# Two thirds of a kernel's query and key transposes from TensorE to the DMA engines, a table built by a product, and wider weight rows

## The chip, the core and the metric

The kernel runs on one core of one Trainium2 chip. The time is the device time of a whole launch in microseconds (us). Some executions are over 1.5% slower than the fastest of the same kernel ("slow" runs, the others are "fast"). Every ratio compares "fast" runs with fast runs.

Engine names: PE is TensorE, PEld its weight load, DVE VectorE, ACT ScalarE, POOL GpSimd, SP (SyncE) the engine that issues most of the DMAs.

## The reference, cut to what matters

```python
# r, k, v: 4 x 8 heads x 768 steps x 48 channels, fp32;  w, u: 8 x 48
for t in range(S):
    cur = k_t (outer) v_t * u
    y[t] = r_t @ (state + cur)
    state = w * state + k_t (outer) v_t
x = y as (3072 tokens, 384)
h = x @ w_in                      # 384 -> 2048
g = maximum(0.01 * h, h)
out = g @ w_out                   # 2048 -> 384, fp32
```

## The kernel before

The recurrence is cut into 24 stages (4 batches of 6 chunks of 128 steps). A stage loads r, k and v (three loads of 192 KB in rows of 192 bytes), scales r and k by decay tables on DVE, transposes both on PE, evicts the transposes on ACT, takes the key-query product, masks it on DVE, multiplies by v and by the carried state, and transposes the result into `xT`. The feed-forward part works on `xT`: first products with w_in, leaky ReLU on ACT, second products with w_out. The first eight tiles have 128 tokens, one per stage; the last four have 512 tokens, so each needs four stages. A small list scheduler in the kernel sorts the operations of each engine by priority before the program is built. Every engine then runs its list strictly in order.

```python
def load(n):                       # three per stage, issued by SyncE; NRAW = 4 buffers
    op("SP", lambda ...: [SP.dma_start(raw[ri][:, :, :], src)], ..., w=[f"{nm}{ri}"])

def front(n):                      # stage n
    ... DVE: qh = r * qdec ;  kh = k * kdec ;  bonus with uw = w * u
    def tr():                      # 8 transposes of 128x128 on TensorE into p_t
        for x, t in ((0, qh), (1, kh)):
            for i in range(NP):
                last = PE.transpose(p_t[:, 512 * x + 128 * i: ... ], t[:, 2 * i:2 * i + 2, :], ident[:, :])
    op("PE", tr, ...)
    op("ACT", lambda: ACT.activation(T, p_t[:, :], AF.Copy), ...)     # eviction, 128x1024
    op("PE", at, ...)              # key-query product p_a <- T
    op("DVE", ...)                 # ATm_0, ATm_1 <- p_a * mask
    ... state update
# [...]
u_tab <- u copied to 128 partitions by one 192 KB load
w_in:  4 loads of fp32, 12 casts on ACT into w_in_sb[:, m, 512 * i: ...]
w_out: 8 casting loads issued by GpSimd, rows of 384 fp32, at WOUT_AT = [3, 3, 4, 4, 5, 5, 6, 6]
```

## Time and profile before

The kernel before takes 194.04 us (193.76 to 194.24, 4 runs). The next lines are from the profile page: PE's busy time with its share of the span of 191.5 us and its instructions, and then the busy tenths of three rows in 40 slices of the span (4.8 us each).

```profile
PE 170.2 (89%) x1768; PEld 113.7 (59%) x1768; DVE 109.3 (57%) x239; ACT 120.5 (63%) x212; POOL 28.8 (15%) x40
...
PE   0249778868899999999999999999999999999994
DVE  2578696977999999999998989910000000000000
DMA  4999999999998989999594010002200121011222
```

PE is full from about a third of the span on. DVE is full from there until two thirds, and the DMA engines are full from the start to slice 20. The stretches view gives the same as busy times in parts of the span; its columns are named in its first line.

```profile
core 0: us, PE busy (x) PEld busy (x) DVE busy (x) ACT busy (x) POOL busy (x), PEclk, DMA share, GB/s
0.00:52.00 52.00, 33.95 (x521) 29.48 (x521) 38.42 (x87) 36.41 (x64) 14.04 (x24) 0.97 1.00 208
...
64.00:92.00 28.00, 28.00 (x315) 18.59 (x313) 27.34 (x59) 15.18 (x28) 5.12 (x6) 1.00 0.98 211
92.00:128.00 36.00, 36.00 (x380) 21.77 (x380) 31.85 (x70) 31.13 (x55) 7.91 (x8) 1.00 0.26 57
```

In the first 52 us PE is busy 34 us, partly with slow instructions (a stage's eight transposes take 1.03 us at 6.9 us and 0.61 us at 53.5 us), while the DMA share is 1.00. (The share counts the time of the packets; they can overlap, so a share above 1 is possible, and it is no exact measure of a full engine.) From 64 to 92 us PE is busy all the time, DVE 27.3 of 28 us, and the DMA share is still 0.98. After 92 us the loads are done (share 0.26). The chain of waits (start, duration, what) agrees:

```profile
22.38 5.80 DMA gT<-in_moe_w_in_dram
28.20 1.68 ACT w_in_sb L484 x3
...
31.49 19.62 DMA raw_v<-in_v_dram x4
...
167.86 20.81 PE p_moe L541 x128
...
188.70 0.49 ACT o_sb L545
```

Early, the chain stands on the load of w_in and on 19.6 us of raw loads; late, it is TensorE alone.

The DMA queue lines of the page give packets, megabytes and the share of the engines' time; the second is GpSimd's queue, which carries w_out.

```profile
q1 hardware_dynamic: 80224, 22.42, 50.6%
q0 software_dynamic: 2176, 1.57, 5.8%
```

The share of w_out is 5.8% of 191.5 us, 11.1 us of all DMA engines.

### The profile page before, as it was taken

Reading aid. Unit: us, or ns where it says so; the run is one execution under the profiler, and the core shown is the slowest. Engines: PE = TensorE matmul, PEld = TensorE weight load, DVE = VectorE, ACT = ScalarE, POOL = GpSimd, SP = SyncE. Lnnn points to the kernel's source line nnn. Section 1 sums busy time; section 2 is a strip of 40 time slices with the busy share of each in tenths; the row PEclk is TensorE's granted clock in tenths of the full one; section 3 lists DMA queues with packets and bytes.
Section 4 is the critical chain, followed back from the end, with each engine's and each line's share of the span. In section 5 each row is a group of like instructions: output and inputs, shape, how many; then the busy total and the mean of one; then the engine's idle time right before and its main releaser. Section 6 shows DMA issues by size and latency. Waiting matters only on the chain.

```text
span 191.5 us, 4244 instructions
## 1 busy us (share of the span) xinstructions
PE 170.2 (89%) x1768; PEld 113.7 (59%) x1768; DVE 109.3 (57%) x239; ACT 120.5 (63%) x212; POOL 28.8 (15%) x40
## 2 busy tenths in 40 slices
PE   0249778868899999999999999999999999999994
PEld 0137667768899676666556656566544654456651
DVE  2578696977999999999998989910000000000000
ACT  3476996668798664554999879851497228922221
POOL 2011153423211111111122121300000000000000
PEclk9999996999999999999999999999999999999999
DMA  4999999999998989999594010002200121011222
GB/s 92 218 213 265 272 245 221 205 200 170 176 213 166 220 173 227 213 238 200 135 202 85 3 41 0 3 0 84 86 0 0 41 82 44 0 39 50 75 86 82
DMA packets 82835, 24.27 MB, mean 127 GB/s; under 512 B 75904, under 2 KB 81280, under 8 KB 82816
## 3 DMA queue, kind: packets, MB, share of 16 engines
q1 hardware_dynamic: 80224, 22.42, 50.6%
q0 software_dynamic: 2176, 1.57, 5.8%
q8 instruction: 14, 0.23, 0.5%
q10 hardware_dynamic: 416, 0.00, 0.1%
q14 instruction: 5, 0.04, 0.1%
HBM read 20.84 MB, written 4.72 MB: 133 GB/s over the span
## 4 chain that ended last, share of the span: by engine, by line
PE 69%; DMA 13%; SPq 11%; DVE 3%; ACT 2%; issue 1%
PE p_moe L541 33%; PE p_moe L521 25%; DMA raw_v<-in_v_dram 10%; SPq L374 8%; PE p_t L404 3%; DMA gT<-in_moe_w_in_dram 3%; PE p_a L415 3%; PE p_y L456 2%; PE p_y L450 2%; PE p_moe L466 1%; SPq L343 1%; SPq L480 1%; PE p_z L428 1%; ACT w_in_sb L484 1%; DVE y_sb L462 1%
## 5 line engine op out<-in xcount | busy, mean ns | idle before, releaser
L521 PE MATMUL p_moe<-xT,w_in_sb 128*128 128x128 bf16 (+1 forms) x576 | 75.4, 280 | 3.0 <-ACT gS L526 1.4
L521 PEld LDWEIGHTS p_moe<-xT,w_in_sb 128*128 128x128 bf16 x576 | 41.9, 102 | 22.5 <-ACT w_in_sb L484 1.9
L541 PE MATMUL p_moe<-w_out_sb,gT 128*128 128x384 bf16 x256 | 42.3, 326 | 0.0
L526 ACT ACTIVATE gT<-p_moe 128x512 bf16<-128x512 f32 x64 | 37.9, 599 | 4.2 <-PE p_moe L521 1.9
L545 ACT ACTIVATE o_sb<-p_moe 128x384 f32<-128x384 f32 x24 | 11.8, 491 | 36.9 <-PE p_moe L541 36.9
L541 PEld LDWEIGHTS p_moe<-w_out_sb,gT 128*128 128x128 bf16 x256 | 25.0, 98 | 16.7
L396 POOL TENSOR_TENSOR vs<-v_sb,s_b 128x384 f32<-128x384 bf16 x24 | 21.4, 893 | 86.2 <-DVE s_b L394 81.3
L409 ACT ACTIVATE qkT<-p_t 128x1024 bf16<-128x1024 bf16 x24 | 24.6, 1026 | 8.1 <-PE p_t L404 7.8
L541 PE MATMUL p_moe<-w_out_sb,gS 128*128 128x384 bf16 x128 | 24.6, 326 | 0.1
L388 ACT ACTIVATE v_sb<-raw_v 128x384 bf16<-128x384 f32 x24 | 12.5, 526 | 11.0 <-DMA raw_v<-in_v_dram 8.3
L526 ACT ACTIVATE gS<-p_moe 128x512 bf16<-128x512 f32 x32 | 18.0, 603 | 1.5 <-PE p_moe L521 1.2
L420 DVE TENSOR_TENSOR ATm_0<-p_a,mask_f 128x512 bf16<-128x512 f32 x24 | 16.4, 684 | 2.0 <-PE p_a L415 1.9
L384 DVE TENSOR_TENSOR q_h<-raw_r,qdec 128x384 bf16<-128x384 f32 x24 | 13.9, 580 | 5.6 <-ACT qdec L351 3.4
L420 DVE TENSOR_TENSOR ATm_1<-p_a,mask_f 128x512 bf16<-128x512 f32 x24 | 16.3, 681 | 0.0
L404 PE MATMUL p_t<-ident,q_h 128*128 128x128 bf16 x96 | 9.8, 227 | 7.3 <-DVE k_h L386 7.3
L386 DVE TENSOR_TENSOR k_h<-raw_k,kdec 128x384 bf16<-128x384 f32 x24 | 15.2, 632 | 0.3 <-DMA raw_k<-in_k_dram 0.3
L462 DVE TENSOR_TENSOR y_sb<-p_y,vs 128x384 bf16<-128x384 f32 x24 | 13.3, 555 | 3.5 <-PE p_y L456 3.3
L541 PEld LDWEIGHTS p_moe<-w_out_sb,gS 128*128 128x128 bf16 x128 | 11.3, 98 | 6.1 <-issue 0.2
L394 DVE TENSOR_REDUCE s_b<-qku 128x8 f32<-128x384 bf16 x24 | 13.1, 547 | 0.2
L470 ACT ACTIVATE xT<-p_moe 128x384 bf16<-128x384 bf16 x24 | 11.7, 489 | 1.6 <-PE p_moe L466 1.6
L404 PEld LDWEIGHTS p_t<-ident,q_h 128*128 128x128 bf16 x96 | 6.9, 102 | 9.2 <-DVE k_h L386 7.5
L415 PE MATMUL p_a<-qkT 64*128 64x128 bf16 x192 | 10.0, 226 | 2.3 <-ACT qkT L409 2.3
(42 smaller groups left out, 146.0 us busy)
## 6 DMA issues: line engine op xcount, KB each, us to landing
raw_r<-in_r_dram SPq DMA_DIRECT2D x24, 192.0 KB, 4.4
raw_k<-in_k_dram SPq DMA_DIRECT2D x24, 192.0 KB, 4.5
raw_v<-in_v_dram SPq DMA_DIRECT2D x24, 192.0 KB, 4.5
out_dram<-o_sb SPq DMA_DIRECT2D x24, 192.0 KB, 1.9
gT<-in_moe_w_in_dram SPq DMA_DIRECT2D x4, 768.0 KB, 5.8
w_out_sb<-in_moe_w_out_dram POOLq DMA_DIRECT2D x8, 192.0 KB, 4.9
w_tab<-in_w_dram SPq DMA_DIRECT2D x1, 192.0 KB, 3.6
u_tab<-in_u_dram SPq DMA_DIRECT2D x1, 192.0 KB, 5.8
```

What stands on the lines that cost most here:

```text
L374: op("SP", lambda src=src, raw=raw: [SP.dma_start(raw[ri][:, :, :], src)], 650, order[0], w=[f"{nm}{ri}"], dma=(f"{nm}{ri}", 16), svc=1000)
L384: op("DVE", lambda: V.tensor_tensor(qh[:, :, 0:D], rr[:, :, :], qdec[:, :, :], ALU.mult), 490, base + 2, w=[f"q{pi}"], r=[f"rr{ri}", "qdec ...
L386: op("DVE", lambda: V.tensor_tensor(kh[:, :, 0:D], rk_[:, :, :], kdec[:, :, :], ALU.mult), 490, base + 3, w=[f"k{pi}"], r=[f"rk{ri}", "kde ...
L396: op("POOL", lambda: G.tensor_tensor(vs[di][:, :, :], vv[:, :, :], s_b[di][:, :].unsqueeze(2).to_broadcast([128, H, D]), ALU.mult), 790, b ...
L404: last = PE.transpose(p_t[:, 512 * x + 128 * i:512 * x + 128 * i + 128], t[:, 2 * i:2 * i + 2, :].rearrange("p h e -> p (h e)"), ident[:, :])
L409: op("ACT", lambda: ACT.activation(T[:, :, :, :].rearrange("p a i t -> p (a i t)"), p_t[:, :], AF.Copy), 910, base + 9, w=[f"T{di}"], r=[g ...
L415: last = PE.matmul(p_a[p][:, 128 * i:128 * i + 128], T[64 * p:64 * p + 64, 1, i, :], T[64 * p:64 * p + 64, 0, i, :], start=True, stop=True)
L420: op("DVE", lambda p=p: V.tensor_tensor(ATm[di][p][:, :, :], p_a[p][:, :].rearrange("p (i t) -> p i t", t=L), mask_f[:, :].unsqueeze(1).to ...
L462: op("DVE", lambda: V.tensor_tensor(y_sb[di][:, :], p_y[:, 0:DM], vs[di][:, :, :].rearrange("p h d -> p (h d)"), ALU.add), 490, base + 15, ...
L521: op("PE", lambda m=m, fb=fb, gr=gr: PE.matmul(p_moe[gr.bank][:, nt * (fb % per):nt * (fb % per) + nt], w_in_sb[:, m, 128 * fb:128 * fb + ...
L526: op("ACT", lambda f0=f0, gr=gr: ACT.activation(gb[:, f0:f0 + per, :], p_moe[gr.bank][:, :].rearrange("p (f t) -> p f t", t=nt), AF.Lrelu) ...
L541: op("PE", lambda q=q, fb=fb, gr=gr: PE.matmul(p_moe[gr.bank][:, 0:DM], gb[:, fb, 128 * q:128 * q + 128], w_out_sb[:, fb, :], start=(fb == ...
```

## The change

It does four things:

1. From stage eight on (`NXQ = 8`), q and k are transposed by a DMA issued from SyncE instead of by PE. This saves the ACT eviction too. From the same stage on, a stage's loads wait until k of two stages earlier is done (`GATE = 2`).
2. u is loaded as one row and spread over the partitions by a one-row product on PE.
3. w_out is loaded in four DMAs whose rows hold four neighbouring rows (6144 bytes). This permutes the hidden channels, so w_in's columns are permuted in its casts.
4. There are four preparation buffers instead of three, three transpose buffers instead of two, and new ranks, priorities and DMA times for the scheduler. So every engine's order of work changes too. `FILL` and `NXY` are set so that they do nothing.

```diff
-WOUT_AT = [3, 3, 4, 4, 5, 5, 6, 6]
-NPREP = 3
+NXQ = 8 ; GATE = 2 ; NT = 3
+WOUT_AT = [3, 4, 5, 6]
+CAST = [20, 118, 160, 218]
+NPREP = 4
[...]
-    op("SP", lambda: [SP.dma_start(u_tab[:, :, :], dram_ap(u, 0, [[0, 128], [D, H], [1, D]]))], ...)
+    op("ACT", lambda: [ACT.dma_start(u_row[:, :], u.rearrange("h d -> (h d)").unsqueeze(0))], ...)
+    op("PE", lambda: PE.matmul(p_moe[gu.bank][:, 0:DM], ones_f[0:1, :], u_row[:, :], ...), ...)
[...]
             op("SP", lambda src=src, raw=raw: [SP.dma_start(raw[ri][:, :, :], src)], 650, order[0],
-               w=[f"{nm}{ri}"], dma=...)
+               w=[f"{nm}{ri}"], after=[f"k{(n - GATE) % NPREP}"] if n >= NXQ else [], dma=...)
[...]
+        if n < NXQ:
             op("PE", tr, ...) ; op("ACT", ... AF.Copy ...)        # as before
+        else:
+            op("SP", lambda: [SP.dma_start_transpose(T..., qk_h[pi]...)], 650, base + RANK["T"], ...)
[...]
-    wo_view = moe_w_out.rearrange("(s p) c -> p s c", p=128)
+    wo_view = moe_w_out.rearrange("(g p j) c -> p g j c", p=128, j=4)
[...]
-            op("ACT", ... w_in_sb[:, m, CH * i:CH * i + CH] <- w_st[i][:, m, :] ...)
+            op("ACT", ... w_in_sb[...].rearrange("p (j q) -> p j q", j=4)
+                       <- w_st[i][:, m, :].rearrange("p (q j) -> p j q", j=4) ...)
```

More of the change, by code (lines that the diff above doesn't have):

```diff
@@ L28 @@
 NRAW = 4
-WIN_AT = [0, 1, 2, 3]
-WOUT_AT = [3, 3, 4, 4, 5, 5, 6, 6]
-NPREP = 3
+FILL = (0.0, 0.0, 215.0)
+NT = 3
+GATE = 2
+NXQ = 8
+NXY = 24
+WIN_AT = [0, 1, 2, 3]
+WOUT_AT = [3, 4, 5, 6]
+CAST = [20, 118, 160, 218]
+RANK = {"q": 2, "k": 3, "v": 4, "bonus": 5, "vs": 7, "T": 8, "Tev": 9, "A": 10, "mask": 11, "kv": 10, "Z": 12, "S": 12,
+        "qs": 14, "av": 14, "y": 15, "xt": 16, "xev": 17}
+NPREP = 4
 NGT = 3
@@ L37 @@
 SLACK = 250
-DMA_LEAD = 1300
-DMA_TAIL = 700
+DMA_LEAD = 1800
+DMA_TAIL = 600
 class Op:
@@ L150, in schedule @@
             if not ready[e]:
+                if e == "PE" and FILL[0] <= free[e] and t < FILL[1] and t - free[e] > 2 * FILL[2]:
+                    o = self.filler(held, free[e])
+                    if o is not None:
+                        o.start, o.end = free[e], free[e] + o.dur
+                        free[e] += o.dur
+                        order[e].append(o)
+                        continue
                 free[e] = t
@@ L190, in schedule, with filler @@
         return order
+    def filler(self, held, t):
+        z = self.writer["zeros"]
+        if z.start is None or z.end > t:
+            return None
+        for b, g in enumerate(held["moe"]):
+            if g is None or (g.last.start is not None and g.last.end <= t):
+                gr = Group("moe")
+                gr.bank = b
+                o = self.op("PE", lambda: self.fill_fn(b), FILL[2], 0, w=[gr], r=["zeros"], grp=gr)
+                o.users = []
+                if g is not None:
+                    o.deps.add(g.last)
+                held["moe"][b] = gr
+                return o
+        return None
     def sync(self, nc, ctx):
@@ L284, in bass_rwkv5_eagle__then__act_leaky_relu_kernel @@
     kdec = SB("kdec", [128, H, D], FP32)
-    u_tab = SB("u_tab", [128, H, D], FP32)
+    u_row = SB("u_row", [1, DM], FP32)
     wt = SB("wt", [128, NP], FP32)
@@ L297, in bass_rwkv5_eagle__then__act_leaky_relu_kernel @@
     v_sb = [SB(f"v_sb{i}", [128, H, D]) for i in range(NPREP)]
-    q_h = [SB(f"q_h{i}", [128, H, E]) for i in range(NPREP)]
-    k_h = [SB(f"k_h{i}", [128, H, E]) for i in range(NPREP)]
+    qk_h = [SB(f"qk_h{i}", [128, 2, H, E]) for i in range(NPREP)]
+    q_h = [t[:, 0, :, :] for t in qk_h]
+    k_h = [t[:, 1, :, :] for t in qk_h]
     qk = [SB(f"qk{i}", [128, H, D]) for i in range(2)]
@@ L303, in bass_rwkv5_eagle__then__act_leaky_relu_kernel @@
     vs = [SB(f"vs{i}", [128, H, D], FP32) for i in range(2)]
-    qkT = [SB(f"qkT{i}", [128, 2, NP, L]) for i in range(2)]
+    qkT = [SB(f"qkT{i}", [128, 2, NP, L]) for i in range(NT)]
     ATm = [[SB(f"ATm{i}_{p}", [128, NP, L]) for p in range(2)] for i in range(2)]
@@ L321, in bass_rwkv5_eagle__then__act_leaky_relu_kernel @@
     p_z = PS("p_z")
+    zeros = SB("zeros", [128, 512])
     P = Prog({"moe": NMOE, "t": 1})
     op = P.op
+    P.fill_fn = lambda b: PE.matmul(p_moe[b][:, :], zeros[:, 0:128], zeros[:, :], start=True, stop=True)
+    op("DVE", lambda: V.memset(zeros[:, :], 0.0), 200, -101, w=["zeros"])
     op("ACT", lambda: ACT.preload_act_table_set("natural_log_exp_and_others"), 1300, -100, w=["acttab"])
@@ L333, in bass_rwkv5_eagle__then__act_leaky_relu_kernel @@
     op("SP", lambda: [SP.dma_start(w_tab[:, :, :], dram_ap(w, 0, [[0, 128], [D, H], [1, D]]))], 650, -100,
-       w=["w"], dma=("w", 16), svc=530)
+       w=["w"], dma=("w", 16), svc=900)
     op("DVE", lambda: V.memset(wt[:, :], 1.0), 70, -100, w=["wt"])
@@ L342, in bass_rwkv5_eagle__then__act_leaky_relu_kernel @@
     op("ACT", wt_dma, 1300, -99, w=["wt"], dma=("wt", 32), svc=300)
-    op("SP", lambda: [SP.dma_start(u_tab[:, :, :], dram_ap(u, 0, [[0, 128], [D, H], [1, D]]))], 650, 1.5,
-       w=["u"], dma=("u", 16), svc=530)
+    op("ACT", lambda: [ACT.dma_start(u_row[:, :], u.rearrange("h d -> (h d)").unsqueeze(0))], 650, -98.9,
+       w=["u"], dma=("u", 16), svc=100)
+    gu = Group("moe")
+    op("PE", lambda: PE.matmul(p_moe[gu.bank][:, 0:DM], ones_f[0:1, :], u_row[:, :], start=True, stop=True), 1300, -90,
+       w=[gu], r=["u", "ones"], grp=gu)
     op("DVE", lambda: V.tensor_reduce(trs[:, :], mask_f[:, :], AX.X, ALU.add), 220, -95, w=["trs"], r=["mask"])
@@ L360, in bass_rwkv5_eagle__then__act_leaky_relu_kernel @@
                                              AF.Exp, scale=float(L)), 250, -49, w=[f"wlm{p}"], r=["wt"])
-    op("DVE", lambda: V.tensor_tensor(uw[:, :, :], w_tab[:, :, :], u_tab[:, :, :], ALU.mult), 490, 3.5, w=["uw"],
-       r=["w", "u"])
+    op("DVE", lambda: V.tensor_tensor(uw[:, :, :], p_moe[gu.bank][:, 0:DM].rearrange("p (h d) -> p h d", d=D),
+                                      w_tab[:, :, :], ALU.mult), 490, -80, w=["uw"], r=["w", gu], grp=gu)
     for i in range(NPREP):
@@ L374, in load @@
             op("SP", lambda src=src, raw=raw: [SP.dma_start(raw[ri][:, :, :], src)], 650, order[0],
-               w=[f"{nm}{ri}"], dma=(f"{nm}{ri}", 16), svc=1000)
+               w=[f"{nm}{ri}"], after=[f"k{(n - GATE) % NPREP}"] if n >= NXQ else [], dma=(f"{nm}{ri}", 16), svc=1000)
             order[0] += 1
@@ L383, in front @@
         qh, kh = q_h[pi], k_h[pi]
-        op("DVE", lambda: V.tensor_tensor(qh[:, :, 0:D], rr[:, :, :], qdec[:, :, :], ALU.mult), 490, base + 2,
+        op("DVE", lambda: V.tensor_tensor(qh[:, :, 0:D], rr[:, :, :], qdec[:, :, :], ALU.mult), 490, base + RANK["q"],
            w=[f"q{pi}"], r=[f"rr{ri}", "qdec"], lock=True)
-        op("DVE", lambda: V.tensor_tensor(kh[:, :, 0:D], rk_[:, :, :], kdec[:, :, :], ALU.mult), 490, base + 3,
+        op("DVE", lambda: V.tensor_tensor(kh[:, :, 0:D], rk_[:, :, :], kdec[:, :, :], ALU.mult), 490, base + RANK["k"],
            w=[f"k{pi}"], r=[f"rk{ri}", "kdec"], lock=True)
-        op("ACT", lambda: ACT.activation(vv[:, :, :], rv[:, :, :], AF.Copy), 420, base + 4, w=[f"v{pi}"],
+        op("ACT", lambda: ACT.activation(vv[:, :, :], rv[:, :, :], AF.Copy), 420, base + RANK["v"], w=[f"v{pi}"],
            r=[f"rv{ri}", "acttab"])
-        op("DVE", lambda: V.tensor_tensor(qk[di][:, :, :], qh[:, :, 0:D], kh[:, :, 0:D], ALU.mult), 270, base + 5,
+        op("DVE", lambda: V.tensor_tensor(qk[di][:, :, :], qh[:, :, 0:D], kh[:, :, 0:D], ALU.mult), 270, base + RANK["bonus"],
            w=[f"qk{di}"], r=[f"q{pi}", f"k{pi}"], lock=True)
-        op("DVE", lambda: V.tensor_tensor(qku[di][:, :, :], qk[di][:, :, :], uw[:, :, :], ALU.mult), 270, base + 5,
+        op("DVE", lambda: V.tensor_tensor(qku[di][:, :, :], qk[di][:, :, :], uw[:, :, :], ALU.mult), 270, base + RANK["bonus"],
            w=[f"qku{di}"], r=[f"qk{di}", "uw"], lock=True)
-        op("DVE", lambda: V.tensor_reduce(s_b[di][:, :], qku[di][:, :, :], AX.X, ALU.add), 470, base + 6,
+        op("DVE", lambda: V.tensor_reduce(s_b[di][:, :], qku[di][:, :, :], AX.X, ALU.add), 470, base + RANK["bonus"],
            w=[f"s{di}"], r=[f"qku{di}"])
@@ L397, in front @@
                                           s_b[di][:, :].unsqueeze(2).to_broadcast([128, H, D]), ALU.mult), 790,
-           base + 7, w=[f"vs{di}"], r=[f"s{di}", f"v{pi}"], lock=True)
+           base + RANK["vs"], w=[f"vs{di}"], r=[f"s{di}", f"v{pi}"], lock=True)
+        T, ti = qkT[n % NT], n % NT
         gt = Group("t")
@@ L406, in tr @@
             return last
-        op("PE", tr, 450, base + 8, w=[gt], r=[f"q{pi}", f"k{pi}", f"qpad{pi}", f"kpad{pi}", "ident"], grp=gt)
-        T = qkT[di]
-        op("ACT", lambda: ACT.activation(T[:, :, :, :].rearrange("p a i t -> p (a i t)"), p_t[:, :], AF.Copy), 910,
-           base + 9, w=[f"T{di}"], r=[gt], grp=gt)
+        if n < NXQ:
+            op("PE", tr, 450, base + RANK["T"], w=[gt], r=[f"q{pi}", f"k{pi}", f"qpad{pi}", f"kpad{pi}", "ident"], grp=gt)
+            op("ACT", lambda: ACT.activation(T[:, :, :, :].rearrange("p a i t -> p (a i t)"), p_t[:, :], AF.Copy), 910,
+               base + RANK["Tev"], w=[f"T{ti}"], r=[gt], grp=gt)
+        else:
+            op("SP", lambda: [SP.dma_start_transpose(T[:, :, :, :].rearrange("p a i t -> p (a i) t"),
+                                                     qk_h[pi][:, :, :, :].rearrange("p a h e -> p (a h e)"))], 650,
+               base + RANK["T"], w=[f"T{ti}"], r=[f"q{pi}", f"k{pi}", f"qpad{pi}", f"kpad{pi}"], dma=(f"T{ti}", 16), svc=1500)
         def at():
@@ L417, in at @@
             return last
-        op("PE", at, 330, base + 10, w=["pa0", "pa1"], r=[f"T{di}"], banks=["a0", "a1"])
+        op("PE", at, 330, base + RANK["A"], w=["pa0", "pa1"], r=[f"T{ti}"], banks=["a0", "a1"])
         for p in range(2):
@@ L422, in front @@
                                                   mask_f[:, :].unsqueeze(1).to_broadcast([128, NP, L]), ALU.mult),
-               630, base + 11, w=[f"A{di}{p}"], r=[f"pa{p}", "mask"], banks=[f"a{p}"])
+               630, base + RANK["mask"], w=[f"A{di}{p}"], r=[f"pa{p}", "mask"], banks=[f"a{p}"])
         if c < NC - 1:
@@ L431, in kv @@
                 return last
-            op("PE", kv, 230, base + 10, w=["pz"], r=[f"k{pi}", f"kpad{pi}", f"v{pi}"], banks=["z"])
+            op("PE", kv, 230, base + RANK["kv"], w=["pz"], r=[f"k{pi}", f"kpad{pi}", f"v{pi}"], banks=["z"])
             pz = p_z[:, 0:DM].rearrange("p (i e) -> p i e", e=2 * D)
@@ L435, in front @@
             if c == 0:
-                op("DVE", lambda: V.tensor_tensor(s_bd[nxt][:, :, :], pz, wlm[:, :, :], ALU.mult), 490, base + 12,
+                op("DVE", lambda: V.tensor_tensor(s_bd[nxt][:, :, :], pz, wlm[:, :, :], ALU.mult), 490, base + RANK["Z"],
                    w=[f"sb{nxt}"], r=["pz", "wlm0", "wlm1"], banks=["z"])
@@ L439, in front @@
                 op("DVE", lambda: V.tensor_tensor(z_st[zi][:, :, :], pz, s_bd[cur][:, :, :], ALU.add), 490,
-                   base + 12, w=[f"z{zi}"], r=["pz", f"sb{cur}"], banks=["z"])
+                   base + RANK["Z"], w=[f"z{zi}"], r=["pz", f"sb{cur}"], banks=["z"])
                 op("DVE", lambda: V.tensor_tensor(s_bd[nxt][:, :, :], z_st[zi][:, :, :], wlm[:, :, :], ALU.mult),
-                   290, base + 12, w=[f"sb{nxt}"], r=[f"z{zi}", "wlm0", "wlm1"], lock=True)
+                   290, base + RANK["S"], w=[f"sb{nxt}"], r=[f"z{zi}", "wlm0", "wlm1"], lock=True)
     def back(n):
@@ L446, in back @@
         pi, di, sc, base = n % NPREP, n % 2, n % 3, n * 100
-        T, vv = qkT[di], v_sb[pi]
+        T, ti, vv = qkT[n % NT], n % NT, v_sb[pi]
         def qs():
@@ L459, in back @@
         if c > 0:
-            op("PE", qs, 200, base + 14, w=["py"], r=[f"T{di}", f"sb{sc}"], banks=["y"])
-        op("PE", av, 330, base + 14, w=["py"], r=[f"A{di}0", f"A{di}1", f"v{pi}"], banks=["y"])
+            op("PE", qs, 200, base + RANK["qs"], w=["py"], r=[f"T{ti}", f"sb{sc}"], banks=["y"])
+        op("PE", av, 330, base + RANK["av"], w=["py"], r=[f"A{di}0", f"A{di}1", f"v{pi}"], banks=["y"])
         op("DVE", lambda: V.tensor_tensor(y_sb[di][:, :], p_y[:, 0:DM], vs[di][:, :, :].rearrange("p h d -> p (h d)"),
-                                          ALU.add), 490, base + 15, w=[f"y{di}"], r=["py", f"vs{di}"], banks=["y"])
+                                          ALU.add), 490, base + RANK["y"], w=[f"y{di}"], r=["py", f"vs{di}"], banks=["y"])
         def xt():
@@ L468, in back @@
         gx = Group("moe")
-        op("PE", xt, 170, base + 16, w=[gx], r=[f"y{di}", "ident"], grp=gx)
-        op("ACT", lambda: ACT.activation(xT[:, :, L * n:L * n + L],
-                                         moe16(gx)[:, 0:DM].rearrange("p (m t) -> p m t", t=L), AF.Copy), 370,
-           base + 17, w=[f"x{n}"], r=[gx], grp=gx)
+        if n < NXY:
+            op("PE", xt, 170, base + RANK["xt"], w=[gx], r=[f"y{di}", "ident"], grp=gx)
+            op("ACT", lambda: ACT.activation(xT[:, :, L * n:L * n + L],
+                                             moe16(gx)[:, 0:DM].rearrange("p (m t) -> p m t", t=L), AF.Copy), 370,
+               base + RANK["xev"], w=[f"x{n}"], r=[gx], grp=gx)
+        else:
+            op("SP", lambda: [SP.dma_start_transpose(xT[:, :, L * n:L * n + L], y_sb[di][:, :])], 650, base + RANK["xt"],
+               w=[f"x{n}"], r=[f"y{di}"], dma=(f"x{di}", 16), svc=700)
     CH = DFF // 4
     wi_view = moe_w_in.rearrange("(m p) c -> p m c", p=128)
-    wo_view = moe_w_out.rearrange("(s p) c -> p s c", p=128)
+    wo_view = moe_w_out.rearrange("(g p j) c -> p g j c", p=128, j=4)
     def weights_in(i):
@@ L483, in weights_in @@
         for m in range(NSL):
-            op("ACT", lambda m=m: ACT.activation(w_in_sb[:, m, CH * i:CH * i + CH], w_st[i][:, m, :], AF.Copy), 520,
-               20 + i, w=[f"win{i}_{m}"], r=st + ["acttab"])
+            op("ACT", lambda m=m: ACT.activation(
+                w_in_sb[:, m, CH * i:CH * i + CH].rearrange("p (j q) -> p j q", j=4),
+                w_st[i][:, m, :].rearrange("p (q j) -> p j q", j=4), AF.Copy), 520,
+               CAST[i], w=[f"win{i}_{m}"], r=st + ["acttab"])
     def weights_out(i, after):
-        op("POOL", lambda: [G.dma_start(w_out_sb[:, 2 * i:2 * i + 2, :], wo_view[:, 2 * i:2 * i + 2, :])],
-           1000, 130 + 100 * i, w=[f"wout{i}"], after=after, dma=(f"wout{i}", 16), svc=1330)
+        op("POOL", lambda: [G.dma_start(w_out_sb[:, 4 * i:4 * i + 4, :], wo_view[:, i, :, :])],
+           1000, 130 + 100 * i, w=[f"wout{i}"], after=after, dma=(f"wout{i}", 16), svc=2100)
     def loads(n):
@@ L538, in g2 @@
             oi[0] += 1
-            ready = [f"{gk}_{fb}" for fb in range(NFB)] + [f"wout{j}" for j in range(8)]
+            ready = [f"{gk}_{fb}" for fb in range(NFB)] + [f"wout{j}" for j in range(4)]
             for fb in range(NFB):
```

## The prediction

> **What bounds it now.** The chain of waits has two parts. Until about 52 us it is input: SyncE issuing loads, a w_in load, and 19.6 us of raw loads ending at 51.1 us. From 63.4 to 188.7 us it is TensorE without a gap; the windows view shows PE busy 4.00 of 4.00 us in every stretch from 64 to 188 us. Counted by that chain's issue slots (q/k transposes 0.45 us a stage, a 512-wide product 0.216, a 384-wide one 0.163), PE's work is about 160 us; 28 us are idle, nearly all before 52 us. Close behind: VectorE is 95 to 100% busy from 48 to 124 us (109 us, about 4.5 us a stage), and the DMA engines are full until 92 us. From 64 to 92 us they are busy 27.4 us with 22 raw loads and 6 stores; a store costs about 0.53 us in the tail, so a raw load about 1.09 us, 3.3 us a stage.
>
> **What changes.**
> - PE loses 16 q/k transposes, 16 x 0.45 = 7.1 us. ScalarE loses 16 evictions of 1.03 us, but is off the chain there.
> - DMA gains 16 transposes of 256 KB. The Trainium skill, "DMA: Bandwidth & Descriptors", section "Latency and other measured facts", gives a DMA transpose 261 GB/s, more when contiguous: my estimate is 1.0 us each, perhaps 1.5. No run shows it yet.
> - The u table goes (about 1.1 us of DMA, ahead of the first v).
> - w_out: 11.1 us of DMA time (5.8% of the span) in small packets becomes 512 rows of 6 KB; I expect 2 to 4 us saved while loads bind. The w_in casts read with a stride: no change expected.
> - Loads from stage eight wait for k of two stages earlier, and the transpose is issued behind them, so it lands 5 to 7 us after k. Three buffers and 11 us of PE work ordered between stages seven and eight cover that.
>
> **On the path.** Stage seven's value product (52.3 us before) should come at about 49 us. The order then has 11 us of PE work to stage eight, so 60 us; 65 us to the last value product, 4.35 us a stage; 48 us of feed-forward after it, plus 2.8 us of tail: 177 us of span without a PE stall. But VectorE needs 4.5 us a stage, and DMA 3.3 + 1.0 + about 0.35 for stores = 4.65, or 5.1 with a slow transpose. So DMA becomes the pace-setter and PE, in fixed order, waits 5 to 11 us in all for transposed tiles and masks: 182 to 188 us. Most of the 7 us is kept, and 2 to 4 us come from the earlier start.
>
> **Prediction:** 184.5 us, 178.5 to 190.5 holding it 8 times in 10. Faster by over 2%: 0.82; within 2%: 0.13; slower: 0.05.
>
> **What would show it.** ScalarE down about 16 us; PE transposes in 8 stages only. DMA share near 1.0 to about 125 us instead of 92; the last value product at 130 to 137 us, not 125.5, followed by 48 us rather than 63. PE waits of a few us on transposed tiles. Transposes 4 to 7 us from issue to landing. Stage zero's v 1 to 2 us earlier.
>
> **What would make it wrong.** A transpose taking over 2.5 us of all DMA engines, or blocking loads behind it: the pace passes 6 us a stage and the time returns to 194 or above. SyncE, in one order, standing on a store that waits for ScalarE while a load is due. Or cheap transposes (0.7 us), giving 178 to 180 us.

## The result and the profile after

The changed kernel took 187.28 us (185.98 to 187.71, 4 runs) beside 194.04 us for the kernel before. The ratio is 0.9641, with a 95% interval of 0.9592 to 0.9691. A ratio here is the mean time of one kernel's fast runs over that of the other's of the same rounds, so it is not quite the ratio of the medians. On two further chips the ratio was 0.979 (0.971 to 0.987) and 0.969 (0.963 to 0.976). So the kernel is 2 to 4% faster, and the chip matters by more than the interval of one chip says.

The same lines of the page after the change:

```profile
PE 162.6 (88%) x1632; PEld 105.7 (57%) x1642; DVE 113.7 (62%) x242; ACT 111.7 (61%) x196; POOL 25.7 (14%) x36
...
PE   0448488796999999999998999999999999999993
DVE  2388758795999899999999999998600000000000
DMA  3999999999659999999999989797000220012122
```

PE is busy 7.6 us less (ten of its matmul records are missing from the second trace, so this is a little too much). The DMA row is nearly full for 28 slices (of 4.6 us, the span is 184.3 us) rather than 20, with a dip in slices 11 and 12, and DVE stays full until slice 28. The stretches:

```profile
0.00:52.00 52.00, 34.35 (x521) 28.84 (x522) 36.69 (x87) 41.91 (x64) 10.38 (x20) 0.97 0.94 203
...
64.00:92.00 28.00, 27.79 (x338) 19.39 (x337) 27.12 (x53) 16.65 (x33) 5.24 (x6) 1.00 1.07 219
92.00:128.00 36.00, 35.24 (x345) 20.24 (x349) 34.80 (x74) 22.66 (x44) 7.38 (x7) 1.00 0.99 188
```

From 92 to 128 us the DMA share rose from 0.26 to 0.99; DVE, the DMA engines and PE are now all near their limit at once, and PE still is busy 63 of the 64 us from 64 to 128. A fourth resource is near its limit as well: SyncE, which issues the loads, the transposes and the stores one after the other. Its issues, added up from the timeline, fill 53.9 of the 60 us from 56 to 116 us, and 57.1 us in two later runs of this kernel, against 36.5 us before the change. The early stretch got no better: in the first 52 us PE is busy 34.4 instead of 34.0 us, and ACT 41.9 instead of 36.4 us. The chain shows ACT there (its lines again are start, duration, what):

```profile
16.51 3.05 ACT w_in_sb L533 x3
...
23.66 2.05 ACT w_in_sb L533 x2
...
30.76 3.04 ACT w_in_sb L533 x3
...
35.65 8.15 DMA raw_v<-in_v_dram
...
160.56 20.82 PE p_moe L592 x128
...
181.40 0.49 ACT o_sb L596
```

Between 16 and 34 us, casts of w_in take 3 us of the chain for three, or 2 us for two. Before, three took 1.7 us. The queue lines and the line of the transposes' issues (count, median us from issue to landing):

```profile
q1 hardware_dynamic: 96976, 26.42, 66.2%
q0 software_dynamic: 576, 1.57, 5.1%
...
qkT<-qk_h SPq DMA_TRANSPOSE x16, 3.7
```

To see where the time went, the first value product of a stage serves as a mark (its first start in the trace). The work of PE between two marks was counted from the instruction order, at the issue slots that the prediction names; this is a count, not a measured time. Its idle time before stage seven also holds what the slow instructions there take beyond their slots.

| from | to | before, us | PE work in it | idle | after, us | PE work in it | idle |
|---|---|---|---|---|---|---|---|
| start | stage 7 | 52.3 | 26.1 | 26.2 | 53.9 | 28.4 | 25.5 |
| stage 7 | stage 8 | 5.2 | 5.0 | 0.2 | 11.3 | 11.2 | 0.1 |
| stage 8 | stage 20 | 55.9 | 53.9 | 2.0 | 56.3 | 54.4 | 1.9 |
| stage 20 | stage 23 | 12.0 | 11.7 | 0.3 | 11.2 | 10.9 | 0.3 |
| stage 23 | last product | 63.3 | 63.0 | 0.3 | 48.7 | 48.3 | 0.4 |

All idle sums to 29.0 us before and 28.2 us after. PE's work sums to 159.7 and 153.2 us. So of the 7.2 us of span, 6.5 are TensorE work that is gone (7.1 us of transposes less, 0.6 us counted for u more; the trace shows u's product taking 1.6 us in an early stretch where PE waits anyway), and 0.8 us is idle time.

The waits view gives PE's waits from stage eight on directly (who waits for what: us in total, times, longest). For transposed tiles this trace shows none. Two further runs of the changed kernel on other chips (after_again and after_third below) show these:

```profile
PE p_a L460 <- DMA qkT<-qk_h: 0.7, 2, 0.5
```

```profile
PE p_a L460 <- DMA qkT<-qk_h: 0.5, 1, 0.5
```

In these two runs the stretch from stage 8 to stage 20 took 58.3 and 57.2 us instead of 56.3, so by the same count PE idles 3.9 and 2.8 us in it.

### The profile page after: what moved, and what is told of

Same layout as the page of the kernel before. It is cut to its first block, busy times and chain, and to the rows that moved or that the text cites. A ratio compares the mean times of both kernels' runs of the same rounds, so it can differ in the third digit from the quotient of the medians.

```text
span 184.3 us, 3981 instructions
## 1 busy us (share of the span) xinstructions
PE 162.6 (88%) x1632; PEld 105.7 (57%) x1642; DVE 113.7 (62%) x242; ACT 111.7 (61%) x196; POOL 25.7 (14%) x36
## 4 chain that ended last, share of the span: by engine, by line
PE 76%; ACT 13%; DMA 6%; DVE 2%; issue 1%
PE p_moe L592 34%; PE p_moe L572 29%; DMA raw_v<-in_v_dram 4%; ACT w_in_sb L533 4%; PE p_a L460 3%; ACT gS L577 2%; PE p_y L501 2%; PE p_y L495 2%; ACT qkT L450 2%; DMA w_tab<-in_w_dram 2%; PE p_moe L511 2%; PE p_t L445 1%; PE p_z L473 1%; PE p_moe L383 1%; ACT xT L516 1%
## 5 line engine op out<-in xcount | busy, mean ns | idle before, releaser
L572 PE MATMUL p_moe<-xT,w_in_sb 128*128 128x128 bf16 (+1 forms) x566 | 74.5, 277 | 5.0 <-ACT w_in_sb L533 2.7
L592 PE MATMUL p_moe<-w_out_sb,gT 128*128 128x384 bf16 x256 | 44.5, 326 | 0.5 <-ACT gT L577 0.5
L436 POOL TENSOR_TENSOR vs<-v_sb,s_b 128x384 f32<-128x384 bf16 x24 | 22.0, 917 | 93.4 <-DVE s_b L434 54.8
L424 DVE TENSOR_TENSOR qk_h<-raw_r,qdec 128x384 bf16<-128x384 f32 x24 | 14.5, 604 | 4.2 <-DMA raw_r<-in_r_dram 4.2
L426 DVE TENSOR_TENSOR qk_h<-raw_k,kdec 128x384 bf16<-128x384 f32 x24 | 15.9, 661 | 0.3 <-ACT wlm L398 0.3
L533 ACT ACTIVATE w_in_sb<-gT 128x512 bf16<-128x512 f32 x12 | 12.7, 1131 | 1.2 <-DMA gT<-in_moe_w_in_dram 1.2
L445 PE MATMUL p_t<-ident,qk_h 128*128 128x128 bf16 x64 | 5.7, 242 | 7.9 <-DVE qk_h L426 7.9
L432 DVE TENSOR_TENSOR qku<-qk,uw 128x384 bf16<-128x384 bf16 x24 | 11.0, 458 | 0.4
```

Source lines behind the costliest of these rows:

```text
L424: op("DVE", lambda: V.tensor_tensor(qh[:, :, 0:D], rr[:, :, :], qdec[:, :, :], ALU.mult), 490, base + RANK["q"], w=[f"q{pi}"], r=[f"rr{ri} ...
L426: op("DVE", lambda: V.tensor_tensor(kh[:, :, 0:D], rk_[:, :, :], kdec[:, :, :], ALU.mult), 490, base + RANK["k"], w=[f"k{pi}"], r=[f"rk{ri ...
L436: op("POOL", lambda: G.tensor_tensor(vs[di][:, :, :], vv[:, :, :], s_b[di][:, :].unsqueeze(2).to_broadcast([128, H, D]), ALU.mult), 790, b ...
L533: op("ACT", lambda m=m: ACT.activation(w_in_sb[:, m, CH * i:CH * i + CH].rearrange("p (j q) -> p j q", j=4), w_st[i][:, m, :].rearrange("p ...
L572: op("PE", lambda m=m, fb=fb, gr=gr: PE.matmul(p_moe[gr.bank][:, nt * (fb % per):nt * (fb % per) + nt], w_in_sb[:, m, 128 * fb:128 * fb + ...
L592: op("PE", lambda q=q, fb=fb, gr=gr: PE.matmul(p_moe[gr.bank][:, 0:DM], gb[:, fb, 128 * q:128 * q + 128], w_out_sb[:, fb, :], start=(fb == ...
```

## The experiments

Twelve kernels were run. Each run is told with its ratio to the kernel before on the same chip.

| run | chip | median us | ratio | 95% interval |
|---|---|---|---|---|
| plaincast | second | 188.11 | 0.958 | 0.954 to 0.962 |
| writestride | second | 203.38 | 1.035 | 1.028 to 1.043 |
| narrow | second | 189.27 | 0.966 | 0.960 to 0.971 |
| pe_all | second | 193.57 | 0.984 | 0.980 to 0.988 |
| after_again | third | 191.13 | 0.979 | 0.971 to 0.987 |
| nogate | third | 193.86 | 0.997 | 0.990 to 1.003 |
| double | third | 212.57 | 1.091 | 1.076 to 1.106 |
| wout_late | third | 187.52 | 0.964 | 0.957 to 0.970 |
| after_third | fourth | 188.46 | 0.969 | 0.963 to 0.976 |
| plaincast_2 | fourth | 189.18 | 0.965 | 0.958 to 0.972 |
| u_only | fourth | 195.95 | 1.010 | 1.003 to 1.017 |
| late_q10 | fourth | 189.34 | 0.970 | 0.962 to 0.978 |

The medians are over all runs of a kernel, four each, but two for writestride and double. Two of plaincast_2's and one of late_q10's were slow runs, which the ratios leave out. All twelve gave correct results.

### Where the gain comes from: all transposes back on TensorE

```diff
-NXQ = 8
+NXQ = 24
```

> The changed kernel with all 24 stages transposed on TensorE (no DMA transposes, and so no load held back); u, w_out, buffers and ranks stay changed. Theory: the gain is TensorE work taken off a TensorE that never rests after 56 us, and the early parts gain nothing: 194 us plus or minus 2. Rival: the gain comes from the early parts (u, w_out): 187 to 189 us.

It took 193.57 us, 0.984 of the kernel before, which took 196.38 us on this chip. The number is in the first theory's range, but its "early parts gain nothing" is not borne out, so the two theories share the result. The transposes are the larger part: plaincast, which has them on the DMA and ran on the same chip, is 5.5 us faster (188.11). It differs from pe_all in three more ways: in the plain casts, whose worth was later found to be too small to resolve; in the hold-back of the loads, which belongs to the DMA transposes; and in the orders that the scheduler makes of it. The remaining 1.6%, 2.8 us between the medians, comes from the other parts of the change together (u, w_out, buffers, ranks). An earlier start is not seen: in pe_all's trace stage seven's value product comes at 56.3 us (the kernel before, traced on another chip, has 52.3).

### The casts: a stride on the read side, none, or on the write side

The first edit below (plaincast) lets the cast read contiguously and moves the permutation into the weight read of the first product. The instruction order on every engine is identical to the changed kernel's.

```diff
-  w_in_sb[:, m, CH * i:CH * i + CH].rearrange("p (j q) -> p j q", j=4) <- w_st[i][:, m, :].rearrange("p (q j) -> p j q", j=4)
+  w_in_sb[:, m, CH * i:CH * i + CH] <- w_st[i][:, m, :]
[...]
-  w_in_sb[:, m, 128 * fb:128 * fb + 128]
+  w_in_sb[:, m, 512 * (fb // 4) + fb % 4:512 * (fb // 4) + 512:4]
```

> The changed kernel with the w_in casts reading contiguously again; the permutation that the wide w_out rows need moves into the weight read of the first product (every fourth column). Instruction order on every engine is identical. Theory: the strided read made each cast 1.13 us instead of 0.62, 12 casts cost 6 us of ScalarE between 10 and 34 us, and ScalarE is in the chain there: casts return to 0.62 us, the value product of stage seven comes 2 to 5 us earlier than 53.9, and the run takes 182 to 185 us. Rival 1: ScalarE had slack, the time stays at 187. Rival 2: a weight load with a stride is slower than 0.10 us and gives all back.

It took 188.11 us, not 182 to 185, and stage seven came at 54.3 us, no earlier than the 53.9 of the changed kernel.

The second (writestride) keeps the permutation in the cast but on the written side.

```diff
-  w_in_sb[...].rearrange("p (j q) -> p j q", j=4) <- w_st[i][:, m, :].rearrange("p (q j) -> p j q", j=4)
+  w_in_sb[...].rearrange("p (j q) -> p q j", j=4) <- w_st[i][:, m, :].rearrange("p (q j) -> p q j", j=4)
```

> The same casts with the stride on the written side instead (contiguous read of fp32, bf16 written 128 elements apart). If only a strided read costs, the cast is 0.62 us and the time as with plain casts; if any stride costs, the cast stays near 1.13 us and the time at 187.

The lines below are those of the weight loads and casts in the view of the tile `w_in_sb`: duration in ns as minimum, median and maximum, then first and last start. The kernel before:

```profile
L521 PEld LDWEIGHTS p_moe<-xT,w_in_sb x576: 95/98/152, 16.8 to 167.3; 128*128 128x128 bf16 x192
...
L484 ACT ACTIVATE w_in_sb<-gT x12: 616/624/651, 11.8 to 29.3; 128x512 bf16<-128x512 f32 x12
```

The changed kernel:

```profile
L533 ACT ACTIVATE w_in_sb<-gT x12: 1094/1128/1158, 10.5 to 32.7; 128x512 bf16<-128x512 f32 x12
```

With plain casts and the strided weight read (plaincast_2):

```profile
L572 PEld LDWEIGHTS p_moe<-xT,w_in_sb x576: 110/113/152, 16.8 to 161.8; 128*128 128x128 bf16 x192
...
L533 ACT ACTIVATE w_in_sb<-gT x12: 612/639/653, 10.4 to 28.2; 128x512 bf16<-128x512 f32 x12
```

With the stride on the written side:

```profile
L533 ACT ACTIVATE w_in_sb<-gT x12: 2473/2772/2800, 10.6 to 46.3; 128x512 bf16<-128x512 f32 x12
```

A cast took 0.62 us, then 1.13 us with a strided read, 0.64 us with the plain read, and 2.77 us with a strided write, which made the run 3.5% slower than the kernel before. The strided weight read costs a median of 113 instead of 98 ns per load, and no wait of PE for a weight load shows in plaincast_2's trace. Neither expectation of writestride held: this cast is far slower with the stride on the written side. Casts this slow do reach the launch: stage seven came at 68.7 us.

The Trainium skill, "SBUF — State Buffer", section "Door 1: The DMA port swizzle (why `[64,N]` ≈ `[32,N]`)", has the rule in a note: SBUF, the core's memory in which the tiles lie, has lines of 16 bytes, "each access that crosses to a new line pays a penalty", and how far one strides for free is put at 4 fp32 or 8 bf16. The casts step 16 bytes, exactly 4 fp32, on the read and 256 bytes on the write. The trace agrees that both pay, 1.8 and 4.4 times the plain cast, but a step of exactly 4 fp32 was not free. No other step was tried, so that the lines are the reason is not shown.

Did the slow casts cost time? plaincast was sent with the changed kernel only later:

> The plain casts again, now beside the changed kernel. Revised theory after the first run: the casts do get 0.5 us shorter each, but ScalarE then waits for raw loads instead, since the DMA engines bind until stage seven; so at most 1 to 2 us faster than the changed kernel on the same chip. Rival (the first theory): 2 to 5 us faster.

> The changed kernel again, as the yardstick of this chip for the three runs beside it: 0.96 to 0.98 of the kernel before.

plaincast_2 reached 0.965 and after_third 0.969 on one chip; the intervals overlap for the most part, which fits the revised theory (at most 1 to 2 us faster). So six microseconds taken from ACT bought nothing that could be resolved. Where most of them went is seen in what ACT's cast of v waits for (us in total, times), first plaincast_2, then the changed kernel on the same chip:

```profile
  DMA raw_v<-in_v_dram: 13.6, 10
```

```profile
  DMA raw_v<-in_v_dram: 5.1, 7
```

ACT's waits for the v loads grew from 5.1 to 13.6 us: ACT became free earlier and then stood waiting for loads. Something was won all the same, and lost later. In these two traces stage seven comes at 52.0 us with plain casts and at 55.2 us in the changed kernel, but stage 20 at 123.3 and 123.7 us: from stage 8 to stage 20 PE waited 1.5 us for a transposed tile and 1.5 us for v's cast with plain casts, 0.5 us and nothing in the changed kernel. An earlier start did not bring an earlier end of the recurrence here.

### The wide rows of w_out

```diff
-    wo_view = moe_w_out.rearrange("(g p j) c -> p g j c", p=128, j=4)
+    wo_view = moe_w_out.rearrange("(g j p) c -> p g j c", p=128, j=4)
     # and plain casts, contiguous weight reads; the order of instructions is that of plaincast
```

> The changed kernel with w_out in narrow rows of 1536 B again (four DMAs), plain casts, contiguous weight loads. Order identical. It differs from plaincast by the wide rows alone. Theory: wide rows save about 2 us of DMA time (software queue 5.1% of the span against 5.8%), so this is 0 to 2 us slower than plaincast. If it is as fast, the wide rows bought nothing and their strided casts were pure loss: then it beats the changed kernel by 2 to 5 us.

It took 189.27 us beside 188.11 for plaincast on the same chip. GpSimd's queue, first with narrow rows, then with wide rows (plaincast):

```profile
q0 software_dynamic: 2112, 1.57, 5.8%
```

```profile
q0 software_dynamic: 576, 1.57, 4.9%
```

That is 5.8% of 189.5 us against 4.9% of 186.3 us, so the wide rows save 1.9 us of DMA time, as this run's expectation had it and just below the 2 to 4 us of the prediction. The medians differ by 1.2 us. The intervals of the two ratios overlap slightly, so the sign is likely and the size is not settled.

### The u change alone

The kernel before, with only the u row and its product.

```diff
-    op("SP", ... u_tab <- u, 128 copies ...)
+    op("ACT", ... u_row <- u ...)
+    op("PE", ... p_moe <- ones_f[0:1, :] x u_row ...)
```

> The kernel before with the u change alone: one row of u loaded, spread over 128 partitions by a TensorE product. Theory: it takes one 192 KB load (about 1.1 us) out of full DMA engines in the first stage, and adds a product of 1.6 us that VectorE waits for; about 1 us faster, between 0 and 2. Rival: the early gain of about 3 us in the run with all transposes on TensorE came from u: 2 to 3 us faster.

It is 1% slower than the kernel before (0.3 to 1.7%), so neither expectation held. The first cast of v did come earlier, at 7.2 instead of 9.5 us. But the timeline (start, duration, engine, what, idle before and its releaser) shows a new wait:

```profile
8.21 1.64 PE L346 MATMUL p_moe<-u_row,ones_f 1*128 1x384 f32 x2
...
9.89 0.56 DVE L364 TENSOR_TENSOR uw<-p_moe,w_tab 128x384 bf16<-128x384 f32 x1 [2.31 <-PE p_moe L346]
```

The product of one fp32 row with 384 columns runs as two PE instructions that take 1.64 us, and DVE stands 2.3 us until it is done. The stage-zero value product starts at 12.89 us, against 12.96 before: what the load gave, the product took. The edit also lets the scheduler reorder everything after it, so the 1% itself is not explained by this wait.

### What the hold-back does

```diff
-  after=[f"k{(n - GATE) % NPREP}"] if n >= NXQ else []
+  after=[f"k{(n - GATE) % NPREP}"] if n >= 99 else []
```

> The changed kernel without the wait that holds a stage's loads back (they wait only for their raw buffer, four stages deep, as before the change). Theory: loads of later stages then fill the DMA queues ahead of each transpose, so issue to landing of a transpose grows from 3.7 us to 6 us or more, the key-query products and masks come late, and the time rises by 2 to 6 us over the changed kernel. Rival: the total DMA work is the same, loads that run ahead only shift it, and the time stays within 1 us (or falls, since no load waits for VectorE).

> The changed kernel itself, to stand on the same chip as the runs sent with it and to show how much its ratio to the kernel before moves from chip to chip. Expected 0.955 to 0.97 of the kernel before.

The changed kernel came to 0.979 here, a little outside its expected 0.955 to 0.97. Without the hold-back the kernel took 193.86 us, 2.7 us longer than the changed kernel on the same chip, and no longer faster than the kernel before. The size was as expected, the mechanism was not. The transposes' time from issue to landing is no longer than in the changed kernel; nogate first, then the changed kernel (minimum, median, maximum):

```profile
DMA to landing us min/median/max: 2.7/3.6/5.4
```

```profile
DMA to landing us min/median/max: 2.7/3.7/5.8
```

The wait sits ahead of the issue. The first lines are the timeline of nogate around the first transposed stage, the second of the changed kernel:

```profile
53.56 0.55 DVE L426 TENSOR_TENSOR qk_h<-raw_k,kdec 128x384 bf16<-128x384 f32 x1
...
54.88 2.03 SPq L414 DMA_DIRECT2D raw_v<-in_v_dram  x2
...
59.63 1.66 SPq L414 DMA_DIRECT2D raw_k<-in_k_dram  x1
...
61.33 1.51 SPq L453 DMA_TRANSPOSE qkT<-qk_h  x1
```

```profile
53.75 0.55 DVE L426 TENSOR_TENSOR qk_h<-raw_k,kdec 128x384 bf16<-128x384 f32 x1
...
55.36 0.72 SPq L414 DMA_DIRECT2D raw_v<-in_v_dram  x1
...
56.13 1.88 SPq L453 DMA_TRANSPOSE qkT<-qk_h  x1
```

In nogate k of stage eight is done at 54.1 us, but SyncE is issuing loads for later stages, each of which holds it for 0.7 to 1.7 us (an issue that meets no other load takes 0.4 us; that the queue is full is the likely reason, which the trace does not show), and comes to the transpose at 61.3 us. In the changed kernel k is done at 54.3 us and the transpose is issued at 56.1 us. Over stages 8 to 19 the time from k's end to the transpose's issue was 6.6 to 13.8 us in nogate, and at most 5.6 us in the changed kernel (6.6 us in its run on the same chip as nogate). One engine issues loads and transposes in one order; holding loads back lets the transpose go before the loads of later stages. It does not give that engine free time: from 56 to 116 us SyncE's issues fill 57.0 of 60 us in nogate and 57.1 us in the changed kernel on the same chip. (Without the wait the scheduler also lays out the other engines' orders anew, so 2.7 us is the effect of both.)

### What a DMA transpose costs

```diff
+            op("SP", lambda: [SP.dma_start_transpose(T2 <- the same qk_h[pi])], ...)   # a second one, never read
```

> Every DMA transpose is issued twice, the second into a buffer that nobody reads: 16 more transposes. Theory: DMA and TensorE are level in this phase (DMA share 1.0 and PE 3.95 of 4.00 us from 56 to 116 us), so DMA time added comes out as time: at 1.0 to 1.6 us each the run is 12 to 25 us longer, PE stands idle, and the DMA share stays near 1. Rival: DMA still has room and VectorE or PE sets the pace: below 4 us longer. Caveat: each extra issue also holds SyncE for about 1.7 us.

The run took 212.57 us, 21.4 us more than the changed kernel on the same chip: 1.34 us for each added transpose. The stretches of the phase with transposes, first double, then the changed kernel (after_again):

```profile
56.00:116.00 60.00, 43.96 (x428) 28.58 (x429) 36.77 (x78) 23.36 (x46) 6.92 (x8) 0.83 0.97 193
116.00:172.00 56.00, 54.31 (x450) 29.93 (x453) 32.47 (x66) 30.82 (x57) 6.25 (x8) 1.00 0.67 139
```

```profile
56.00:116.00 60.00, 57.74 (x601) 36.15 (x604) 56.93 (x113) 34.75 (x69) 11.23 (x12) 1.00 1.09 200
```

The time grew by what the theory said (12 to 25 us), and from 56 to 116 us PE falls to 44 of 60 us: the phase had little room for another transpose. But that the DMA engines were what had no room is not shown. Their share is 0.97, less than the 1.09 of the changed kernel, and 0.67 in the second stretch. Each added transpose also holds SyncE for 1.2 us or more. PE's granted clock was 0.83 in that stretch (1.00 in the changed kernel), which may add to the time. The scheduler also gave PE 26.6 instead of 11.3 us of work between stages seven and eight. So part of the 21.4 us is order and waiting, not transfer. From the queue's shares, the time of the hardware queue's packets rose from 68.2% of 187.3 us to 67.4% of 212.3 us, 15.4 us or 0.96 us per transpose; between pe_all and plaincast, 49.7% of 192.9 us and 68.2% of 186.3 us give 1.95 us. So a transpose of 256 KB costs 1 to 2 us of the DMA engines by packet time (an estimate from these shares), and 1.34 us in elapsed time here, with all that the run adds.

### Towards a faster version

Since the DMA engines bind until stage seven, and w_out is first used after it, w_out may come later. The kernel has plain casts and:

```diff
-WOUT_AT = [3, 4, 5, 6]
+WOUT_AT = [5, 6, 7, 8]
```

> Plain casts as in plaincast, and the four w_out loads two stages later (at stages five to eight instead of three to six). Theory: until stage seven the raw loads and w_out compete for full DMA engines while TensorE idles, and w_out is first used after stage seven; w_out later lets stages four to seven arrive earlier, so first products run earlier: 1 to 4 us faster than plaincast. Rival: w_out then lands when second products are due, and TensorE waits there: same or slower.

It took 187.52 us, beside 191.13 us for the changed kernel on the same chip; the ratios are 0.964 and 0.979, and their intervals just do not meet. The value product of stage seven starts at 51.5 us, against 55.0 us in the changed kernel on the same chip (53.9 and 55.2 us on two others) and 54.3 and 52.0 us in the two plain-cast runs. This version beats the kernel before and the changed kernel on its chip. That it beats plaincast by 1 to 4 us, as expected, is not shown: plaincast has 0.958 and 0.965 on other chips, and no run stood beside it. The further step did not pay visibly:

```diff
-NXQ = 8
+NXQ = 10        # on top of wout_late
```

> As wout_late (plain casts, w_out at stages five to eight), and the DMA transposes begin at stage ten instead of eight. Two transposes (2 x 1.3 us of DMA) leave the stretch where the late w_out now competes with them, for 0.9 us more PE work. If the transposes' wait at SyncE in that stretch (5 to 9 us) was costing PE, this is 0 to 2 us faster than wout_late's 0.964 of the kernel before; if PE work is all that counts, it is about 1 us slower.

It has 0.970 on another chip, with an interval that overlaps wout_late's, so neither of its two expectations is decided.

## Why the prediction was right or wrong, point by point

- **The total.** 184.5 us was predicted with a range of 178.5 to 190.5; 187.28 us was measured. "Faster by over 2%" came true. Two terms of opposite sign were mis-sized and nearly cancelled (stage seven 4.9 us later than predicted, the stall after it 2 to 8 us shorter), so that the middle came so close is partly luck.
- **"PE loses 16 q/k transposes, 7.1 us", mostly kept: right.** PE's counted work fell by 6.5 us in all and the span by 7.2 us. With all transposes back on PE, the run was 5.5 us slower than plaincast.
- **"2 to 4 us come from the earlier start", stage seven at about 49 us: wrong.** It came at 53.9 us. PE's idle time before it fell only from 26.2 to 25.5 us. The loads saved (u, w_out) were real: stage zero's v was cast at 7.1 instead of 9.5 us, and the wide rows saved 1.9 us. But the u product took back what the u load gave, and the chain moved onto the casts. Taking away the casts' cost moved it back to the raw loads (6.7 and 4.9 us of v loads between 29 and 42 us in plaincast_2's chain). pe_all nevertheless shows 2.8 us for all other parts together on its chip. Which of buffers, ranks and rows gives that is not settled.
- **"The w_in casts read with a stride: no change expected": wrong.** They went from 0.62 to 1.13 us, 6 us of ACT, so ACT's busy time fell by 8.8 us and not by about 16. That this cost the launch little is not because the stride is free: without it ACT waited for loads instead.
- **"DMA becomes the pace-setter" at 4.65 to 5.1 us a stage: the pace is right, the pace-setter not shown.** The loads of stages 10 to 22 were issued 4.75 us apart (13 issues of r from 54.3 to 111.3 us). The DMA share was 1.07 and 0.99 in the two stretches from 64 to 128 us. But DVE was busy 61.9 of these 64 us, and SyncE issued for 54 to 57 of the 60 us from 56 to 116. At their shortest in the trace (0.37 us a load, 1.28 a transpose, 0.33 a store) SyncE's five issues of a stage would take an estimated 2.7 us, so most likely it was being slowed by something else; but no run issued the transposes from another engine, so this rival stays untested.
- **"PE waits 5 to 11 us in all for transposed tiles": wrong.** By the waits view PE waited 0, 0.7 and 0.5 us for transposed tiles in the three traces of the changed kernel. By the count it idled about 2.6 us in all after stage eight, no more than before the change (up to about 4.6 us on the other chips). The step that failed was comparing that pace with an average of 4.35 us of PE work a stage. From stage 8 to stage 20 the order holds 54.4 us of work, 4.53 us a stage; only the last three stages, which no more loads follow, hold 3.6 us each. So only the difference of 4.69 us taken and 4.53 us of work, twelve times, was lost in this trace.
- **"The last value product at 130 to 137 us, followed by 48 us": right**, 132.7 us and 48.7 us to the last product.
- **The transpose: "1.0 us each, perhaps 1.5", from the skill's 261 GB/s: in range.** 1.34 us in elapsed time, 1 to 2 us by packet time. "It lands 5 to 7 us after k" was too short for half of the 16 transposes, which landed up to 9.9 us after k: 3.7 us (median) from issue to landing, after up to 5.6 us at SyncE before the issue.
- **"SyncE, in one order, standing ... while a load is due"**, named as a risk, is in part what the hold-back avoids. nogate shows it coming true with the roles turned round: a transpose due, loads in front.

## What to carry to other kernels

Work moved off the engine that binds paid nearly in full here (6.5 of 7.1 us) because the receiving side stayed level with the fixed order; count the receiving side's pace against the work that the order has between two marks, not against an average that includes a tail. Count the engine that issues the DMAs among the resources: here it was almost always issuing. When several things are issued by one in-order engine, look at the time before the issue as well as at the time to landing: holding bulk loads back was worth 2.7 us here, together with the orders that came with it, and the landing time showed nothing. Relieving an engine in a phase that another resource binds (6 us of casts here) can turn its busy time into a wait, so look for what the chain would stand on next.

## What the Trainium skill lacked or had wrong

- "SBUF — State Buffer": the note on 16-byte lines gives 4 fp32 as how far a stride is free, but a read with a step of exactly 4 fp32 was not. Nor does the note say what a stride costs, or that the sides differ. A 128x512 cast on ACT took 0.62 us plain, 1.13 us with fp32 read 16 bytes apart, and 2.77 us with bf16 written 256 bytes apart.
- "DMA: Bandwidth & Descriptors", section "Latency and other measured facts": 261 GB/s for a DMA transpose (about 350 to 400 when contiguous) is neither confirmed nor refuted. 256 KB from SBUF to SBUF took 0.96 to 1.95 us by packet time, an estimated 273 to 134 GB/s, and 1.34 us in elapsed time beside raw loads, which works out to 196 GB/s, with the caveats told above.
- The same page, section "DMA Transpose (X-bar)", has no time for what the issue costs the issuing engine on this chip (a comparison of chip generations elsewhere on the page gives sequencer cycles only): 1.3 to 3.8 us of SyncE for each transpose here (median 1.7 us), while an unhindered load took 0.4 us. No page was found that sizes how long a transpose behind loads of the same engine waits before its issue (6.6 to 13.8 us in nogate, stages 8 to 19), where the time to landing (3.6 us) does not show it.
- "TensorE: Matmul & The Clock Gate", section "Weight-path perf modes — Fast Weight Load (FWL) and DoubleRow", allows a column step in the weight read but gives no cost: a step of four bf16 columns made a 128x128 weight load 113 instead of 98 ns (medians).
